# One fused kernel of attention and two feed-forward layers: weight splitting moved to GpSimd, gate splitting moved to VectorE, and a planner that counts a shared port

## The chip, the cores and the metric

The kernel runs on one core of one Trainium2 chip. The metric is the device time of one execution in microseconds (us), as the median of several runs. The engines are named as in the profile: PE (TensorE, matmul), PEld (its weight loads), DVE (VectorE), ACT (ScalarE), POOL (GpSimd) and SP (the queue that issues DMAs).

## The reference

```python
scores = scale * q @ k^T + bias(i, j)          # B=2, H=8, S=576, D=64
attn   = softmax(scores) @ v                   # -> x: 1152 tokens x 512
h = x @ w_in;  g = s * relu(h)**2 + b;  x = g @ w_out           # layer 1, 512 -> 2048 -> 512
h = x @ w_in;  g = h * tanh(log1p(exp(min(h, 20))));  out = g @ w_out   # layer 2, same sizes
```

The bias is a small two-layer network of the distance between positions. The weights arrive as 64-bit floats and are put together from two 32-bit words on the chip.

## The kernel before, in words

Every matmul of the two layers has 32-bit precision made of three products of a rounded format: each operand is taken apart into a high part (a rounding copy) and a low part (the operand minus the high part), and the product is high x high + low x high + high x low. So each weight block and each gate block needs a copy and a subtraction.

A layer is worked through as 48 tiles: three passes j of 384 tokens, and in each pass 16 blocks f of 128 hidden features. A tile has its hidden products (L788, 12 matmuls into a PSUM bank `h`, of which there are four), its gates, and its sums (L865, 12 matmuls in layer 1 and 9 in layer 2, added up over the pass in the PSUM banks `y`, of which there are four). Layer 1 uses four `y` banks in a pass, layer 2 three. The hidden products of a tile stand several tiles ahead of its sums on PE.

In layer 2 the gates of a tile are six DVE operations and three ACT operations in a chain: `least` (DVE, L806, reads PSUM), `exp` (ACT, L809), `both` (DVE, L813), `log` and `over` (ACT, L817, L820), then `one`, `times`, `newton`, `gate` (DVE, L823, L826, L829, L832); `times` is the last that reads the bank `h`. Then ACT makes the high part `gh` (L842) and POOL or DVE the low part `gl` (`minus`, L157). In layer 1 it is `relu` (ACT, L798), `square` (DVE, L801), `gh` (ACT) and `gl` (DVE).

The weights of layer 2 are prepared during the third pass of layer 1, 32 blocks of 128 x 512 (16 `wi` for the hidden products, 16 `wo` for the sums). For each: a DMA, `widen` (two ACT operations, L138 and L139), `join` (DVE, L144), `high` (a copy: on ACT for `wi`, on DVE for `wo`, L163), `low` (`minus` on DVE, L157). The buffer `wf` that `widen` fills has two copies each for `wi` and `wo` and comes free with `low`.

At the end of layer 1's last pass, `scaled_sum` (DVE, L876) reads the four `y` banks, which frees them for layer 2, and at the end of each pass of layer 2 `out_left` (ACT, L888) and `out_right` (DVE, L891) copy the sums out of their banks to `ob`.

The order of the instructions on every engine is set by a planner in the kernel (`Plan.run`): each operation is a task with a cost in us, a rank, what it comes after, and which buffers it holds. The planner starts the task that can start earliest. A task whose `port` is set can't overlap another such task: these are all of POOL's, and on DVE `bias_row` and `join`.

Of the kernel before, what the change touches and what calls it, by code (L numbers as in the profile page):

```python
# [10 lines left out]
F32 = mybir.dt.float32  # L11
# [10 lines left out]
def attention_bias_then_two_moe(ctx: ExitStack, tc: tile.TileContext, ins, out):  # L22
    nc = tc.nc
    q, k, v = ins["q"], ins["k"], ins["v"]
# [17 lines left out]
    NF = FF // P  # L42
    TB = 384
    NB = NT // TB
# [30 lines left out]
    HLEAD = 25  # L75
# [5 lines left out]
    DEAL = 6  # L81
    WEARLY = ("i0", "i1", "o0", "i2", "o1", "i3", "o2", "o3")
    FILL = 4
    LASTV = 2
    LXRANK = -78
    CUT = 0
    FRANK = 32
# [2 lines left out]
    GRANK = -190  # L90
    PRANK = -66
    VRANK = 1
    BIG = 3.0e38
    SD = S // DEAL
    scale = 1.0 / float(np.sqrt(D))
# [25 lines left out]
    class Weights:  # L121
# [26 lines left out]
            self.wlo = self.pool[0].tile([P, KD * P], F32R, tag=f"w{self.nm}l", name=f"wl{self.name}")  # L148
            copy(SPLIT["io".index(self.nm)], self.whi, self.wf.bitcast(F32))

        def low(self):
            minus(nc.vector, self.wlo, self.wf.bitcast(F32), self.whi)
            self.put[self.nm] = self.whi, self.wlo

    def minus(engine, out, x, y):

        engine.tensor_tensor(out, x, y.bitcast(F32), op=ALU.subtract)  # L157
# [338 lines left out]
    class Task:  # L496
        def __init__(self, engine, us, rank, f, args, after, takes, lag, mb):
            self.engine, self.us, self.rank, self.f, self.args = engine, us, rank, f, args
            self.after, self.takes, self.lag, self.mb = list(after), list(takes), lag, mb
            self.start = self.end = None  # L500
            self.behind, self.past = [], []

            self.port = engine == "POOL" or f.__name__ in ("bias_row", "join") and engine == "DVE"

    class Hold:
        def __init__(self, what):
# [2 lines left out]
    class Plan:  # L509
# [5 lines left out]
        def add(self, engine, us, rank, f, *args, after=(), takes=(), mb=0.0):  # L515
            t = Task(engine, us, rank, f, args, after, takes, self.LAGS[engine], mb)
            self.tasks.append(t)
            return t
# [60 lines left out]
    add = plan.add  # L579
# [24 lines left out]
    for x, G in enumerate(gorder):  # L604
        n, first, step = GFIRST
        at = -200 + 8 * x if x < NFIRST else 10 * (first + step * x if x < n else first + step * n + GSTEP * (x - n))
        w = side(G)[0]
        hs = [Hold("r") for a in range(RI)]
        rs = [
            add(*(("ACT", 0.0008 * w + 0.1) if row_engine(G, a) == "a" else ("DVE", 0.0007 * w + 0.05)), at - 15 + a,  # L610
                bias_row, G, a, after=[], takes=[hs[a]])
# [9 lines left out]
        for c0, c1 in bias_pieces(G):  # L621
            h1 = Hold("one")
            p = add("PE", 0.00167 * (c1 - c0) + 0.14, at, bias_products, G, c0, c1, after=rs, takes=[h1])
# [12 lines left out]
    for n, (key, i) in enumerate(firsts.items()):  # L636
        st = stacks[key]
        at = 10 * (i - QLEAD if n >= Q0 else -5 + n)
        packs = []
        for nm in "qk":  # L640
# [5 lines left out]
            who = "a" if n < PACK0 else "p"  # L646
# [4 lines left out]
        for what in range(3):  # L651
            h1 = Hold("one") if big is None or what == 2 else hold
            t = add("PE", 0.3 if what == 2 else 0.55, at + what, st.turn, what, big,
                    after=([packs[what][1]] if what < 2 else [p1 for _, p1 in packs]) + ts[-1:], takes=[] if h1 is hold and what else [h1])
            ts.append(t)
            if what == 2:
                for hn, _ in packs:
                    hn.users.append(t)
            who = PUTS[what]
            p = add(*(("ACT", 0.28 if what == 2 else 0.46) if who == "a" else ("DVE", 0.28 if what == 2 else 0.57)), at + what + 1,  # L660
                    st.put, what, who, after=[t, *puts[:1]])
# [7 lines left out]
    for i, u in enumerate(units):  # L669
        at = 10 * i  # L670
        if u.b == 0:
            for n in range(u.n):
                h = Hold("nb")
                after = [*issued[-1:], *([scored[i - NLEAD]] if i >= NLEAD else []), *(stores[G] for G in range(u.q0 // (RI * RI), (u.q0 + u.w) // (RI * RI)))]
                nbh[u.hp, u.t, n] = h, add("SP", 1.1 if u.both else 0.55, at - (80 if i > 1 else 400), load_bias, u.hp, u.t, u.heads(n), after=after,
                                           takes=[h], mb=0.29)
# [6 lines left out]
        for n in range(u.n):  # L683
            h, load = nbh[u.hp, u.t, n]
            hs = Hold("s")
# [13 lines left out]
        t = add("PE", 0.62 * u.n, at + RANK["turn"], u.turn, after=ds, takes=[hp, hr])  # L699
# [9 lines left out]
        p = add("PE", 1.24 if u.n == 2 else 0.73, at + RANK["V"], u.values, after=[kp, kr, valued[u.hp, u.b]], takes=[ho])  # L709
# [39 lines left out]
    whave, wused = {}, {}  # L749

    def add_w(L, f, nm, at, early):
        w = Weights(wpa if f < EARLY else wpb, L, f, nm)
        two = "2" if nm == "o" and not early else ""
        if two:
            def load():
                w.st = stg[1]
                w.load()
        else:
            load = w.load
        hr, hf, hw = Hold("wraw" + two), Hold("wf" + two), Hold(f"w{'a' if f < EARLY else 'b'}{nm}")  # L760
        new = [] if early else [opened]
        t = add("SP", 0.42, at - 20, load, after=[ended, *(new if two else [])], takes=[hr], mb=0.52)
        t = add("ACT", 1.12, at, w.widen, after=[t], takes=[hf])
        t = add("DVE", 0.6, at + 1, w.join, after=[t])
        hr.users.append(t)
        t = add(*(("ACT", 0.52) if SPLIT["io".index(nm)] == "a" else ("DVE", 0.34)), at + 2, w.high, after=[t, *new], takes=[hw])
        t = whave[L, f, nm] = add("DVE", 0.6, at + 3, w.low, after=[t])
        hf.users.append(t)
        wused[L, f, nm] = hw.users

# [126 lines left out]
    ready = {(0, j): lows[j] for j in range(NB)}  # L897
# [8 lines left out]
    for n, (L, j, f) in enumerate((L, j, f) for L in range(2) for j in range(NB) for f in range(NF)):  # L906
# [9 lines left out]
        if n < FILL:  # L916
            hs = []
            for c in range(KD):
                hs.append(add("PE", 0.53, 10 * (len(units) + FRANK + 5 * f), blk.hidden, (c,), after=[lasts, wi, *hs, *ready[L, j]],
                              takes=[] if c else [hh]))  # L920
        else:
            hs = [add("PE", 2.08, at - HLEAD, blk.hidden, after=[lasts, wi, *ready[L, j]], takes=[hh])]
        in_turn(hs[0], "h")
        wused[L, f, "i"] += hs
        if not WHOLE:
# [111 lines left out]
```

## Time and profile before

| What | us |
|---|---|
| median of 3 runs (618.38 to 619.24) | 618.52 |
| the profiled execution, whole | 619.38 |
| its span, first to last instruction | 617.6 |
| PE busy / DVE busy | 592.8 / 470.2 |
| ACT busy / POOL busy | 381.1 / 123.4 |

Attention takes the first 204 us of the span, layer 1 runs to about 416 us and layer 2 from there to the end. The granted PE clock is 0.999 of full speed. PE is at work 96% of the span. A line of the timeline gives start, duration, engine, line, operation, what it writes and reads and how many instructions are merged in it; in brackets stand the idle time of the engine before it and what ended that.

### The profile page before, as it was taken

Reading aid. Unit: us, or ns where it says so; the run is one execution under the profiler, and the core shown is the slowest. Engines: PE = TensorE matmul, PEld = TensorE weight load, DVE = VectorE, ACT = ScalarE, POOL = GpSimd, SP = SyncE. Lnnn points to the kernel's source line nnn. Section 1 sums busy time; section 2 is a strip of 40 time slices with the busy share of each in tenths; the row PEclk is TensorE's granted clock in tenths of the full one; section 3 lists DMA queues with packets and bytes.
Section 4 is the critical chain, followed back from the end, with each engine's and each line's share of the span. In section 5 each row is a group of like instructions: output and inputs, shape, how many; then the busy total and the mean of one; then the engine's idle time right before and its main releaser. Section 6 shows DMA issues by size and latency. Waiting matters only on the chain.

```text
span 617.6 us, 12029 instructions
## 1 busy us (share of the span) xinstructions
PE 592.8 (96%) x4416; PEld 520.7 (84%) x4416; DVE 470.2 (76%) x1048; ACT 381.1 (62%) x797; POOL 123.4 (20%) x183
## 2 busy tenths in 40 slices
PE   3988999999999999999999999999999999999996
PEld 1444687778888999999999999997898789989984
DVE  5999978877896699634223889899888777787885
ACT  3766877778998899623123788754555444545543
POOL 2223335343344000000000000001222212222120
PEclk9999999999999999999999999999999999999999
DMA  5786756646543678700000377420000100010001
GB/s 121 249 250 204 215 155 179 196 131 201 181 142 103 203 227 281 246 1 1 1 0 13 100 244 242 154 69 1 2 0 1 51 2 2 0 52 1 2 1 51
DMA packets 47083, 65.97 MB, mean 107 GB/s; under 512 B 12720, under 2 KB 32304, under 8 KB 47024
## 3 DMA queue, kind: packets, MB, share of 16 engines
q1 hardware_dynamic: 46688, 64.81, 34.2%
q8 instruction: 35, 0.57, 0.4%
q10 hardware_dynamic: 336, 0.39, 0.2%
q14 instruction: 24, 0.20, 0.1%
HBM read 51.93 MB, written 13.25 MB: 106 GB/s over the span
## 4 chain that ended last, share of the span: by engine, by line
PE 78%; DVE 14%; ACT 3%; DMA 2%; issue 2%; POOL 1%; SPq 0%; ACTq 0%; DVEq 0%
PE h L788 29%; PE y L865 28%; PE s L405 6%; PE po L467 6%; DVE r L257 5%; PE pp L446 5%; PE bias L267 3%; DMA rawq<-in_q_dram 2%; DVE s L415 1%; DVE r L829 1%; DVE u L823 1%; PE pr L448 1%; DVE n L826 1%; PE t L369 1%; DVE qk L163 1%
## 5 line engine op out<-in xcount | busy, mean ns | idle before, releaser
L157 POOL TENSOR_TENSOR gl<-n,gh 128x384 fp32r<-128x384 f32 x46 | 47.4, 1031 | 291.2 <-ACT gh L842 291.2
L437 POOL TENSOR_SCALAR e<-e,rs 128x576 f32<-128x576 f32 x72 | 55.9, 788 | 91.4 <-DVE rs L433 45.1
L257 DVE TENSOR_SCALAR r<-lx,bl 128x352 f32<-128x352 f32 (+17 forms) x144 | 66.6, 523 | 2.1 <-PE bias L267 1.7
L801 DVE SCALAR_TENSOR_TENSOR u<-h,u 128x384 f32<-128x384 f32 x48 | 26.6, 555 | 52.9 <-ACT u L798 52.8
L788 PE MATMUL h<-yh,wli 128*128 128x384 f32 x192 | 64.8, 337 | 0.0
L788 PE MATMUL h<-yh,whi 128*128 128x384 f32 x192 | 64.7, 337 | 0.0
L788 PE MATMUL h<-yl,whi 128*128 128x384 f32 x192 | 64.7, 337 | 0.0
L788 PE MATMUL h<-xh,whi 128*128 128x384 f32 x192 | 64.6, 336 | 0.0
L788 PE MATMUL h<-xh,wli 128*128 128x384 f32 x192 | 64.5, 336 | 0.0
L788 PE MATMUL h<-xl,whi 128*128 128x384 f32 x192 | 64.4, 336 | 0.0
L425 ACT ACTIVATE e<-s,mn 128x576 f32<-128x576 f32 x72 | 55.5, 772 | 9.7 <-DVE mn L415 7.0
L798 ACT ACTIVATE u<-h 128x384 f32<-128x384 f32 x48 | 23.3, 487 | 58.6 <-PE h L788 58.6
L415 DVE CUSTOM_DVE_ANT_0 s<-s,nb 128x576 f32<-128x576 f32 x72 | 52.4, 751 | 9.2 <-PE s L405 9.0
L817 ACT ACTIVATE r<-n,two 128x384 f32<-128x384 f32 x48 | 29.5, 614 | 38.9 <-DVE n L813 38.9
L823 DVE SCALAR_TENSOR_TENSOR u<-n,r 128x384 f32<-128x384 f32 x48 | 35.2, 733 | 23.0 <-ACT r L820 23.0
L405 PE MATMUL s<-qk 64*128 64x144 f32 (+1 forms) x640 | 49.6, 294 | 1.1 <-DVE mn L415 0.8
L405 PEld LDWEIGHTS s<-qk 64*128 64x128 f32 (+1 forms) x640 | 40.6, 176 | 10.4 <-issue 5.2
L865 PE MATMUL y<-who,gh 128*128 128x512 f32 x144 | 43.9, 399 | 4.5 <-ACT gh L842 1.6
L809 ACT ACTIVATE u<-u 128x384 f32<-128x384 f32 x48 | 25.0, 521 | 34.1 <-DVE u L806 34.1
L865 PE MATMUL y<-gl,who 128*128 128x384 f32 (+1 forms) x192 | 44.5, 338 | 0.0
L865 PE MATMUL y<-gh,wlo 128*128 128x384 f32 (+1 forms) x192 | 44.4, 337 | 0.0
L865 PE MATMUL y<-gh,who 128*128 128x384 f32 (+1 forms) x192 | 44.3, 337 | 0.0
(89 smaller groups left out, 1412.3 us busy)
## 6 DMA issues: line engine op xcount, KB each, us to landing
rawi<-in_moe_w_in_dram SPq DMA_DIRECT2D x32, 512.0 KB, 4.3
rawo<-in_moe_w_out_dram SPq DMA_DIRECT2D x32, 512.0 KB, 4.4
nbias_d<-bo SPq DMA_DIRECT2D x36, 295.5 KB, 2.9
nb<-nbias_d SPq DMA_DIRECT2D x32, 288.0 KB, 3.8
rawq<-in_q_dram SPq DMA_DIRECT2D x8, 288.0 KB, 5.8
rawk<-in_k_dram SPq DMA_DIRECT2D x8, 288.0 KB, 6.3
out_dram<-ob SPq DMA_DIRECT2D x9, 256.0 KB, 2.0
natv<-in_v_dram SPq DMA_DIRECT2D x16, 128.0 KB, 3.6
```

What stands on the lines that cost most here:

```text
L157: engine.tensor_tensor(out, x, y.bitcast(F32), op=ALU.subtract)
L257: engine.tensor_scalar(r, src, bl[:, g : g + 1], 0.0, op0=ALU.add, op1=ALU.max)
L405: nc.tensor.matmul(self.ps[rows, x if self.both else 2 * j + x, o : o + PIECE], st.qk[d, 0, self.q0 : self.q0 + self.w], st.qk[d, 1, c0 : ...
L415: nc.vector.tensor_tensor_reduce(out=self.s[n][:m], in0=self.ps[:m, 2 * n : 2 * n + 2, :HALF], in1=nb[:m].rearrange("p (n j) -> p n j", n= ...
L425: nc.scalar.activation(out=self.e[n][:m], in_=self.s[n][:m].rearrange("p n j -> p (n j)"), func=AF.Exp, bias=self.mn[n][:m], scale=-1.0, a ...
L437: nc.gpsimd.tensor_scalar(self.e[n][:m], self.e[n][:m], self.rs[:m, n : n + 1], 0.0, op0=ALU.mult, op1=ALU.add)
L446: nc.tensor.transpose(self.pp[:, n, c, :m], self.e[n][:m, c * P : c * P + P], ident[:m, :m])
L467: nc.tensor.matmul(self.po[D * j : D * j + D, :w], va[:, c, j, :], p, start=(c == 0), stop=(c == NQ - 1))
L788: nc.tensor.matmul(self.ph, w[:, c * P : (c + 1) * P], x[:, c, :], start=(c == 0 and n == 0), stop=(c == KD - 1 and n == 2),)
L817: nc.scalar.activation(out=self.r, in_=self.n, func=AF.Ln, bias=two)
L823: nc.vector.scalar_tensor_tensor(self.z, self.n, 2.0, self.r, op0=ALU.add, op1=ALU.mult)
L865: nc.tensor.matmul(o, a, c, start=(f == 0 and i == 0), stop=(f == NF - 1 and i == 2))
```

## The change

Four things are changed, the first of them in the planner alone.

- The planner sets `port` for `both`, `one`, `newton` and `gate` on DVE too.
- `low` of the weights: in layer 2 (`LOWS[1] = "pp"`) it runs on POOL, at a planned cost of 1.3; in layer 1 it stays on DVE.
- `LASTV` goes from 2 to 34: the low part `gl` of the last 34 tiles (tiles 14 and 15 of layer 2's first pass, and its second and third pass) runs on DVE, where it was on POOL for all but the last two.
- `TAIL = 15`: the hidden products of the last four tiles have a rank of 40 ahead of their sums (`HLEAD` of 25 plus 15), so four tiles where it was two and a half.

```diff
-    LASTV = 2
+    LASTV = 34
...
+    PORTS = ("bias_row", "join", "both", "one", "newton", "gate")
+
+    LOWS = ("vv", "pp")
+    TAIL = 15
...
-        def low(self):
-            minus(nc.vector, self.wlo, self.wf.bitcast(F32), self.whi)
+        def low(self, who):
+            minus(nc.gpsimd if who == "p" else nc.vector, self.wlo, self.wf.bitcast(F32), self.whi)
...
-            self.port = engine == "POOL" or f.__name__ in ("bias_row", "join") and engine == "DVE"
+            self.port = engine == "POOL" or engine == "DVE" and f.__name__ in PORTS
...
-        t = whave[L, f, nm] = add("DVE", 0.6, at + 3, w.low, after=[t])
+        who = LOWS[L]["io".index(nm)]
+        t = whave[L, f, nm] = add(*(("DVE", 0.6) if who == "v" else ("POOL", 1.3)), at + 3, w.low, who, after=[t])
...
-            hs = [add("PE", 2.08, at - HLEAD, blk.hidden, after=[lasts, wi, *ready[L, j]], takes=[hh])]
+            hs = [add("PE", 2.08, at - HLEAD - (TAIL if n >= 2 * NB * NF - 4 else 0), blk.hidden, after=[lasts, wi, *ready[L, j]], takes=[hh])]
```

The order on all engines is the same as before up to the third pass of layer 1. From there it differs in many places; three follow. A name such as `h1_0_4` is the bank of layer 2 (numbered 1), pass 0, block 4; `y1_0_2` is the sum of layer 2, pass 0, third bank; the last number is a buffer's. Five lines added ahead shift the line numbers: L865 is L870 in the change, L157 is L161.

**DVE at the seam of the two layers.** The rows from the copy of the last but one `wo` to the third `scaled_sum` (`y32_2_e`), before:

```order
L163 CAST who_1_14_5547<-wfo_1_14_5478 128x512
L876 TENSOR_SCALAR y32_2_0_5552<-y0_2_0_4731,s_sb_71,bw_73 128x384
L157 TENSOR_TENSOR wlo_1_14_5548<-wfo_1_14_5478,who_1_14_5547 128x512
L832 TENSOR_TENSOR n1_0_1_5500<-n1_0_1_5500,r1_0_1_5505 128x384
L157 TENSOR_TENSOR yl2_5551<-y32_2_0_5552,yh2_5550 128x384
L163 CAST who_1_15_5584<-wfo_1_15_5528 128x512
L806 TENSOR_SCALAR u1_0_3_5588<-h1_0_3_5464 128x384
L157 TENSOR_TENSOR wlo_1_15_5585<-wfo_1_15_5528,who_1_15_5584 128x512
L876 TENSOR_SCALAR y32_2_1_5592<-y0_2_1_4781,s_sb_71,bw_73 128x384
L813 SCALAR_TENSOR_TENSOR n1_0_2_5594<-u1_0_2_5526 128x384
L157 TENSOR_TENSOR yl2_5551<-y32_2_1_5592,yh2_5550 128x384
L876 TENSOR_SCALAR y32_2_2_5605<-y0_2_2_4812,s_sb_71,bw_73 128x384
```

and in the change:

```order
L167 CAST who_1_14_5535<-wfo_1_14_5469 128x512
L837 TENSOR_TENSOR n1_0_1_5472<-n1_0_1_5472,r1_0_1_5479 128x384
L881 TENSOR_SCALAR y32_2_0_5546<-y0_2_0_4729,s_sb_71,bw_73 128x384
L148 SCALAR_TENSOR_TENSOR wfo_1_15_5523<-rawo_1_15_5447,wfo_1_15_5523 128x512
L161 TENSOR_TENSOR yl2_5545<-y32_2_0_5546,yh2_5544 128x384
L167 CAST who_1_15_5571<-wfo_1_15_5523 128x512
L881 TENSOR_SCALAR y32_2_1_5579<-y0_2_1_4761,s_sb_71,bw_73 128x384
L818 SCALAR_TENSOR_TENSOR n1_0_2_5595<-u1_0_2_5515 128x384
L161 TENSOR_TENSOR yl2_5545<-y32_2_1_5579,yh2_5544 128x384
L881 TENSOR_SCALAR y32_2_2_5600<-y0_2_2_4789,s_sb_71,bw_73 128x384
```

The subtractions `wlo` are gone from this queue; on POOL they now stand between the first `gl` of layer 2 (`wlo_1_13`, `gl1_0_0`, `wlo_1_14`, `gl1_0_1`, `wlo_1_15`, `gl1_0_2`). On PE the hidden products `h1_0_4` have gone from ahead of the last two blocks of layer 1's sums to between layer 1's last sum and layer 2's first; `h1_0_5` still follows that first sum.

**PE at the seam of layer 2's first and second pass.** One row of a group of three or twelve; before:

```order
L865 MATMUL y1_0_2_5609<-who_1_15_5584,gl1_0_15_6107 128x512
L865 MATMUL y1_1_0_6197<-who_1_0_4861,gh1_1_0_6146 128x512
L865 MATMUL y1_1_0_6197<-who_1_0_4861,gl1_1_0_6147 128x512
L865 MATMUL y1_1_1_6206<-who_1_0_4861,gh1_1_0_6146 128x512
L788 MATMUL h1_1_4_6233<-yl1_4721,whi_1_4_4802 128x384
```

and in the change:

```order
L870 MATMUL y1_0_2_5609<-who_1_15_5571,gl1_0_15_6122 128x512
L870 MATMUL y1_1_0_6189<-who_1_0_4838,gh1_1_0_6157 128x512
L870 MATMUL y1_1_0_6189<-who_1_0_4838,gl1_1_0_6158 128x512
L793 MATMUL h1_1_4_6200<-yl1_4718,whi_1_4_4816 128x384
L870 MATMUL y1_1_1_6223<-who_1_0_4838,gh1_1_0_6157 128x512
```

The twelve hidden products of tile 4 have moved ahead of the second sum of the new pass. At the next seam, of the second and third pass, `h1_2_3` has moved the other way: from ahead of the three first sums to behind them.

**PE at the end.** One row of a group of three, six or twelve; before:

```order
L788 MATMUL h1_2_14_7227<-yl2_5551,whi_1_14_5282 128x384
L865 MATMUL y1_2_0_6814<-who_1_11_5410,gl1_2_11_7207 128x512
L865 MATMUL y1_2_0_6814<-who_1_12_5456,gh1_2_12_7245 128x512
L788 MATMUL h1_2_15_7266<-yl2_5551,whi_1_15_5311 128x384
L865 MATMUL y1_2_0_6814<-who_1_12_5456,gl1_2_12_7246 128x512
```

and in the change:

```order
L793 MATMUL h1_2_14_7214<-yl2_5545,whi_1_14_5290 128x384
L870 MATMUL y1_2_0_6794<-who_1_11_5394,gh1_2_11_7209 128x512
L793 MATMUL h1_2_15_7255<-yl2_5545,whi_1_15_5337 128x384
L870 MATMUL y1_2_0_6794<-who_1_11_5394,gl1_2_11_7210 128x512
L870 MATMUL y1_2_0_6794<-who_1_12_5444,gh1_2_12_7240 128x512
```

The hidden products of the last tile, and of the three before it, stand nine matmuls of a sum further ahead.

## Rows read from the trace of the kernel before

**Rows 1.** Busy time of the engines in two stretches, with instruction counts
```profile
core 0: us, PE busy (x) PEld busy (x) DVE busy (x) ACT busy (x) POOL busy (x), PEclk, DMA share, GB/s
345.00:412.00 67.00, 67.00 (x385) 67.00 (x385) 58.91 (x110) 51.91 (x101) 0.00 (x0) 1.00 0.56 173
491.00:541.00 50.00, 50.00 (x252) 45.16 (x251) 37.23 (x70) 24.62 (x48) 11.93 (x12) 1.00 0.00 1
```

**Rows 2.** Timeline of PE at the seam of the two layers
```profile
419.43 0.50 PE L865 MATMUL y<-who,gh 128*128 128x512 f32 x1 [0.43 <-DVE y L876]
...
420.00 0.40 PE L865 MATMUL y<-who,gl 128*128 128x512 f32 x1
421.29 0.50 PE L865 MATMUL y<-who,gh 128*128 128x512 f32 x1 [0.89 <-DVE y L876]
```

**Rows 3.** Timeline of PE at the seam of layer 2's first two passes
```profile
483.74 0.40 PE L865 MATMUL y<-who,gl 128*128 128x512 f32 x1
485.67 0.51 PE L865 MATMUL y<-who,gh 128*128 128x512 f32 x1 [1.53 <-DVE ob L891]
```

**Rows 4.** Timeline of PE at the end
```profile
604.11 0.86 PE L865 MATMUL y<-who,gl 128*128 128x512 f32 x3
...
607.70 0.96 PE L865 MATMUL y<-who,gh 128*128 128x512 f32 x3 [0.65 <-ACT gh L842]
...
611.05 0.50 PE L865 MATMUL y<-who,gh 128*128 128x512 f32 x1 [0.99 <-ACT gh L842]
```

**Rows 5.** The chain that ended last, two tiles' worth in layer 2's third pass
```profile
593.74 2.11 PE h L788 x12
595.86 2.10 PE y L865 x9
```

**Rows 6.** Groups of DVE instructions from 336 to 412 us: count, busy, mean ns
```profile
L157 DVE TENSOR_TENSOR wli<-wfi,whi 128x512 fp32r<-128x512 f32 x15 | 10.3, 687 | 0.0
L144 DVE SCALAR_TENSOR_TENSOR wfi<-rawi,wfi 128x512 int32<-128x512 int32 x14 | 9.7, 692 | 4.2 <-ACT rawi L139 4.1
...
L163 DVE CAST who<-wfo 128x512 fp32r<-128x512 f32 x14 | 5.9, 421 | 0.8 <-PE y L865 0.8
```

**Rows 7.** POOL's gate subtractions: all of them as one group, and two in the timeline
```profile
L157 POOL TENSOR_TENSOR gl<-n,gh 128x384 fp32r<-128x384 f32 x46 | 47.4, 1031 | 291.2 <-ACT gh L842 291.2
...
417.23 1.01 POOL L157 TENSOR_TENSOR gl<-n,gh 128x384 fp32r<-128x384 f32 x1 [3.71 <-ACT gh L842]
...
603.24 1.02 POOL L157 TENSOR_TENSOR gl<-n,gh 128x384 fp32r<-128x384 f32 x1 [2.24 <-ACT gh L842]
```

**Rows 8.** Timeline of DVE at the seam of the two layers
```profile
414.79 0.67 DVE L876 TENSOR_SCALAR y<-y,s_sb,bw 128x384 f32<-128x384 f32 x1
...
417.72 1.07 DVE L157 TENSOR_TENSOR wlo<-wfo,who 128x512 fp32r<-128x512 f32 x1
418.71 0.67 DVE L876 TENSOR_SCALAR y<-y,s_sb,bw 128x384 f32<-128x384 f32 x1
...
420.56 0.68 DVE L876 TENSOR_SCALAR y<-y,s_sb,bw 128x384 f32<-128x384 f32 x1
```

**Rows 9.** Timeline of DVE at the seam of layer 2's first two passes
```profile
481.83 0.56 DVE L832 TENSOR_TENSOR n<-n,r 128x384 f32<-128x384 f32 x1
...
485.19 0.42 DVE L891 COPY ob<-y 128x256 f32<-128x256 f32 x1
```

**Rows 10.** Timeline of DVE and of ACT in the last tiles
```profile
603.61 1.06 DVE L823 SCALAR_TENSOR_TENSOR u<-n,r 128x384 f32<-128x384 f32 x1 [1.09 <-ACT r L820]
604.60 0.54 DVE L806 TENSOR_SCALAR u<-h 128x384 f32<-128x384 f32 x1
605.07 0.54 DVE L826 SCALAR_TENSOR_TENSOR n<-n,h 128x384 f32<-128x384 f32 x1
...
606.57 0.62 ACT L817 ACTIVATE r<-n,two 128x384 f32<-128x384 f32 x1 [0.87 <-DVE n L813]
607.55 0.51 ACT L820 ACTIVATE r<-r 128x384 f32<-128x384 f32 x1
```

## The prediction

> **What bounds the kernel now.** I read the table of stretches first. It shows PE at work without a break from 345 to 412 us and from 491 to 541 us [rows 1]; a tile takes PE 2.11 for its hidden products and 2.10 for its sums, 4.2 us together [rows 5]. So in a layer's steady part PE is the bound, and a change that leaves PE's 4416 matmuls as they are can win only where PE stands still. The timeline of PE shows three such places behind attention, and the reader is to see in each what ended the wait.
>
> At the seam of the two layers PE waits 0.43 and then 0.89 for `scaled_sum` on DVE to free a `y` bank [rows 2]; nine matmuls of a sum in 2.10 start 0.23 apart, and the second wait makes 1.29 of that, so the two cost 0.43 + 1.06 = 1.5 us. At the seam of layer 2's first two passes it waits for `out_right` on DVE, and 1.93 stands where 0.23 would: 1.7 us [rows 3]. At the end it waits 0.65 and 0.99 for the last gates' high parts: 1.6 us [rows 4]. The sum is 4.8 us, the most that the change can give but for restarts (the first matmul behind each wait is some 0.1 longer, 0.50 for 0.40 [rows 2]). Attention and the first two passes of layer 1 keep their order on every engine, so nothing is won or lost ahead of 340 us.
>
> **The end.** In the change the last tile's hidden products come nine matmuls earlier: they end at 604.11 - 2.10 = 602.0, and behind them stand 0.7 (the rest of block 11) and four sums of 2.1 (blocks 12 to 15). So the sums of block 14 begin 4.9 us behind the last hidden products, those of block 15 7.0. Are the gates there by then? DVE starts an operation 0.47 behind the one before it (604.60 and 605.07) where nothing holds it; ACT's `log` takes 0.62 and its others about 0.5 [rows 10]. In the change's order the last tile runs: `least` 0.6, `exp` 0.55, `both` behind two operations of the tile before, done at 2.0; `log` and `over` to 3.2; `one` 3.7; then the `gl` of tile 14, `times`, `newton`, `gate` to 5.7; `gh` 6.2, `gl` 6.8. That is 0.8 ahead of block 15's sums, and tile 14's `gh` comes at about 3.7, 1.2 ahead of its own. The walk has no wait for POOL, since POOL now has nothing to do there; before, `one` was held by it to 1.06 us [rows 10] while POOL's subtraction ran [rows 7]. So I take the whole 1.6 off. If the walk is 1.5 too short, 0.7 of that stays.
>
> **The seam of layer 2's passes.** Twelve matmuls of `h1_1_4` (2.1 us) now stand ahead of the second sum, so PE asks for the bank 2.1 later. Before, the bank came at 485.67, 1.7 late. The copy that frees it (485.19) stood behind the `one` and `times` of tile 2; in the change it stands behind the `gate` of tile 1, which before was over by 482.4 [rows 9]. The wait goes: -1.7. `h1_1_4` needs the bank of `h1_1_0`, whose `times` lies before that `gate`. At the next seam `h1_2_3` no longer covers the copies: the second sum of the third pass now asks for its bank 2.8 us behind the end of the bank's own sum. In between come ACT's half and DVE's half of the copy, 0.4 each [DVE's: rows 9]. I cost that at nothing; if DVE stands as it did at the seam before (bank free 485.6, its sum over nine matmuls ahead of 483.74 [rows 3], by 482.0, so 3.6), it costs 0.8.
>
> **The two last passes.** `gl` moves to DVE for 34 tiles where it was there for two: one more operation of 0.47 per tile. DVE was busy 37.23 us for 12 tiles, 3.1 per tile [rows 1]; with 0.47 more it is 3.6, of 4.2. It also loses the wait for POOL, up to 0.5 per tile. DVE stays off the path; cost nothing, cover 0.6 per tile.
>
> **The weights of layer 2.** DVE loses 32 subtractions of 0.69 [rows 6], 0.60 each in its queue, 19 us in all. But DVE is not the bound in that stretch (58.91 of 67 busy, PE full [rows 1]), so this gives nothing by itself. POOL gets them. Their price is not in the trace: POOL's subtraction of 384 columns takes 1.03 [rows 7], so one of 512 takes between 1.03 (length costs nothing) and 1.37 (in proportion); I take 1.3, nearer to proportion, since DVE's own go 0.55 to 0.69. What matters is that the two engines exclude each other: DVE's subtraction at 417.72 took 1.07 where 0.69 is free [rows 8, 6], and ended 0.55 behind the end of POOL's (418.24 [rows 7]); `one` did the same at 603.61. From that one, POOL gives way about 0.1 ahead of its end, so I count 1.2 held.
>
> In that stretch a tile of 4.2 us meets two `join`s (0.60 each), a `who` copy (0.34, if it needs the port), a `gl` of layer 1 (0.47) and two of POOL's: 1.2 + 0.34 + 0.47 + 2.4 = 4.4 us of port. The planner counts only `join` and POOL's. So DVE and POOL fall 0.2 a tile behind for the nine or so tiles in which both kinds of weights are made, about 2 us; then, with `wo` alone (2.6 a tile), they recover. PE doesn't feel it there: with four `h` banks it asks for a tile's bank three tiles, 12.6 us, behind that tile's hidden products, and `relu` and `square` need little over 1 us of that. Behind a late POOL, `widen` on ACT waits for its `wf` buffer, and `relu` and `gh` queue behind it; those have the same slack.
>
> **The seam of the layers.** This is where lateness would show. PE's hidden products `h1_0_4` now fill 2.1 us between layer 1's last sum and layer 2's first, so the last sums end 2.1 earlier and `scaled_sum` can start at about 412.7 where it stood at 414.79 [rows 8], while PE asks for the second bank as before at 419.0, for the third at 419.7. From the first `scaled_sum` to the end of the third the change has ten operations, 5 us, less the two `wlo` that stood there, plus the holds by POOL: three of its operations fall there, for which I count half, 1.7. From 412.7 that ends at 419, in time; before it ended at 421.2 (the last of [rows 8]). If DVE arrives 2 us late, the third bank is 1.1 late. I take that: 1.5 of waits becomes 1.1, -0.4. Bounds: no wait (-1.5) and, if port time is 0.5 a tile more than counted, +5.
>
> The sum: -1.6 - 1.7 - 0.4 = -3.7, with 0.2 for restarts -3.9. The profiled execution took 619.38, so 615.5; it lies 0.86 above the median, so for the median **614.6 us**.
>
> **The rivals.** *The port is the bound (slower).* If POOL's subtraction holds the port for its whole 1.37 and each change of holder costs another 0.1, a tile needs 2.75 + 2.0 + 0.4 = 5.2 us of port for 4.2 of PE. Over 12 tiles DVE is 12 us late; 1 is slack and some 3 is recovered with `wo` alone, so PE stands 8 us at the layers' seam where it stood 1.5: +6.5 - 3.3 - 0.2 = +3.0, 621.5. The change is slower than before from about 0.8 late per tile on. For it: `wlo` at 1.07; nothing in the trace shows long runs of such neighbours. Against: with `wo` alone it recovers, and `who` waits for PE's sums of the same block anyway. The Trainium skill has a rule on this side: "Perfetto Trace Analysis", section Optimizing Scalar/DVE Operations, warns that moving work between GpSimd and DVE may not help, as they share a read port. By that rule the 19 us that DVE loses come back as waits. The trace agrees as far as the exclusion goes (1.07 for 0.69).
>
> *DVE becomes the bound of the last passes.* DVE idled (50 - 37.23) / 12 = 1.06 a tile [rows 1], in waits for ACT inside the chain. If these stay whole, seven operations of 0.47 and they make 4.35, above 4.2: over 31 tiles 4.7 late, which eats the lead and the gain at the end. Then -1.7 - 0.4: 616.4.
>
> *The waits only move.* DVE has been full at the layers' seam, and PE could wait for the gates of the next tiles in place of the banks. Then each seam keeps its loss: 618.2, no change.
>
> **How the numbers follow.** Forecast 0.62 (613.0 to 616.0 by itself), port 0.14, DVE in the last passes 0.14, waits that move 0.10. A measurement can tell about 0.2%, 1.2 us. Faster: nearly all of the first and most of the third, 0.72; same 0.14; slower 0.14, the port. The range goes from 612.4 (all waits and restarts gone, 1.1 more) to 619.2 (waits that move, and the port's mild cases).
>
> **What would show it.** Right: PE's wait of 1.53 for `ob` gone, the last wait for `gh` gone, the last two passes at 4.2 a tile, `wli` and `wlo` on POOL near 1.3, and a wait for `scaled_sum` of 1 us or less at the seam. Wrong: POOL busy without a break from 345 to 420, DVE's `join` and `gl` near 1 us, and a wait of several us at the first sums of layer 2; or sums of the last passes waiting for `gl` on DVE.

## The result, and the profile after

The changed kernel takes 623.58 us (median of 4 runs, 623.35 to 623.82) where the kernel before took 618.88 beside it (618.38 to 619.46). The ratio is 1.0076, with a 95% interval of 1.0058 to 1.0093: slower by 0.8%, where 614.6 was predicted, faster, with a range that ended at 619.2. The profiled span is 621.6 us, before it was 617.6.

The table of stretches answers to [rows 1]. Columns: stretch, its length, busy time of PE, weight loads, DVE, ACT and POOL (instructions), PE's granted clock, DMA share, GB/s.

```profile
345.00:412.00 67.00, 66.76 (x381) 66.05 (x379) 57.01 (x70) 47.79 (x92) 38.60 (x25) 1.00 0.52 165
491.00:541.00 50.00, 50.00 (x253) 45.20 (x252) 43.05 (x87) 26.43 (x51) 0.00 (x0) 1.00 0.04 17
```

In the last passes DVE now has 43.05 of 50 us where it had 37.23, and PE is still full: that part went as predicted. In layer 1's third pass PE is nearly full too, POOL has gone from 0 to 38.60 us, and DVE, with 40 instructions fewer in this window (70 for 110), is busy almost as long (57.01 for 58.91). It got rid of a third of its operations and of next to none of its time.

PE's timeline at the seam of the two layers answers to [rows 2]. Columns, as in all timelines here: start, duration, engine, line, operation, and in brackets the idle time before it and who ended it.

```profile
412.36 0.44 PE L870 MATMUL y<-gh,who 128*128 128x384 f32 x1 [0.55 <-ACT gh L847]
...
415.52 0.44 PE L793 MATMUL h<-yh,whi 128*128 128x384 f32 x1 [0.47 <-DVE n L831]
...
423.27 0.80 PE L870 MATMUL y<-who,gh 128*128 128x512 f32 x1 [5.37 <-DVE y L881]
...
424.72 0.52 PE L793 MATMUL h<-yh,whi 128*128 128x384 f32 x1
425.04 0.52 PE L793 MATMUL h<-yl,whi 128*128 128x384 f32 x1
...
428.56 0.62 PE L870 MATMUL y<-who,gh 128*128 128x512 f32 x1
...
429.48 0.39 PE L870 MATMUL y<-who,gh 128*128 128x512 f32 x1
```

The sum into the third bank began at 421.29 before [rows 2], now at 429.48, 8.2 us later. PE stands (sits idle) for 5.37 us behind one `scaled_sum`, where it stood 0.43 and 0.89, with two short stands ahead of it. Behind the stand the twelve products of a tile take 428.56 - 424.72 = 3.84 us for 2.11 [rows 5]: they start 0.32 apart, not 0.17 to 0.18. The table of stretches for the seam shows why:

```profile
418.00:423.00 5.00, 0.00 (x0) 0.00 (x0) 4.89 (x9) 2.96 (x6) 1.88 (x3) 0.92 0.00 2
423.00:429.00 6.00, 5.73 (x17) 5.35 (x18) 5.91 (x9) 2.51 (x6) 3.46 (x3) 0.50 0.01 3
429.00:435.00 6.00, 6.00 (x30) 5.28 (x29) 5.17 (x10) 2.98 (x7) 1.02 (x1) 1.00 0.00 0
```

PE has done nothing from 418 to 423, and in the next 6 us the granted clock is 0.50, the lower of its two levels (1.2 GHz); by 429 it is back at 2.4.

DVE's three sums answer to [rows 8]:

```profile
422.55 0.67 DVE L881 TENSOR_SCALAR y<-y,s_sb,bw 128x384 f32<-128x384 f32 x1
...
425.85 0.67 DVE L881 TENSOR_SCALAR y<-y,s_sb,bw 128x384 f32<-128x384 f32 x1
...
428.21 0.68 DVE L881 TENSOR_SCALAR y<-y,s_sb,bw 128x384 f32<-128x384 f32 x1
```

The first is at 422.55 where it stood at 414.79 and was predicted at 412.7. DVE comes 8 us late to the seam, 10 against the forecast. From there to the end of the third sum it takes 428.89 - 422.55 = 6.3 us, as long as the forecast had it (412.7 to 419); so the lateness is made ahead of the seam. Where from, the groups from 336 to 412 us show, the answer to [rows 6] (columns: group, count, busy time, mean ns of one, idle time before them and who ended it); the last two, POOL's, are from 336 to 432:

```profile
L161 DVE TENSOR_TENSOR gl<-u,gh 128x384 fp32r<-128x384 f32 x16 | 18.2, 1137 | 1.7 <-ACT gh L847 1.7
L167 DVE CAST who<-wfo 128x512 fp32r<-128x512 f32 x12 | 12.2, 1016 | 0.3 <-PE y L870 0.3
L148 DVE SCALAR_TENSOR_TENSOR wfi<-rawi,wfi 128x512 int32<-128x512 int32 x14 | 11.6, 825 | 2.5 <-ACT rawi L143 2.2 <-issue 0.4
L148 DVE SCALAR_TENSOR_TENSOR wfo<-rawo,wfo 128x512 int32<-128x512 int32 x12 | 11.5, 962 | 2.4 <-ACT rawo L143 1.2 <-issue 1.1
L806 DVE SCALAR_TENSOR_TENSOR u<-h,u 128x384 f32<-128x384 f32 x15 | 8.3, 554 | 5.3 <-ACT u L803 5.2
...
L161 POOL TENSOR_TENSOR wlo<-wfo,who 128x512 fp32r<-128x512 f32 x16 | 24.9, 1558 | 18.3 <-DVE who L167 18.3
L161 POOL TENSOR_TENSOR wli<-wfi,whi 128x512 fp32r<-128x512 f32 x15 | 22.3, 1485 | 22.3 <-ACT whi L165 14.8 <-DVE u L806 7.4
```

The copy `who` takes 1016 ns in the mean where it took 421, `join` of `wfo` 962 and of `wfi` 825 where 692 stood, layer 1's `gl` 1137 where one takes 0.55 unhindered. Only `square`, which reads one operand from PSUM, keeps its 554. POOL's own operations take 1485 and 1558 in the mean, and 1.29 us where nothing of DVE's holds them.

One tile of this stretch, one of the longest, all engines that matter, the changed kernel:

```profile
395.60 0.56 DVE L806 SCALAR_TENSOR_TENSOR u<-h,u 128x384 f32<-128x384 f32 x1 [0.62 <-ACT u L803]
396.07 0.68 DVE L148 SCALAR_TENSOR_TENSOR wfi<-rawi,wfi 128x512 int32<-128x512 int32 x1
396.67 1.54 DVE L167 CAST who<-wfo 128x512 fp32r<-128x512 f32 x1
398.13 0.68 DVE L148 SCALAR_TENSOR_TENSOR wfo<-rawo,wfo 128x512 int32<-128x512 int32 x1
398.74 1.64 DVE L161 TENSOR_TENSOR gl<-u,gh 128x384 fp32r<-128x384 f32 x1
401.00 0.56 DVE L806 SCALAR_TENSOR_TENSOR u<-h,u 128x384 f32<-128x384 f32 x1 [0.62 <-ACT u L803]
...
396.17 1.76 POOL L161 TENSOR_TENSOR wli<-wfi,whi 128x512 fp32r<-128x512 f32 x1 [1.60 <-ACT whi L165]
398.29 1.68 POOL L161 TENSOR_TENSOR wlo<-wfo,who 128x512 fp32r<-128x512 f32 x1 [0.37 <-DVE who L167]
...
400.47 0.49 ACT L803 ACTIVATE u<-h 128x384 f32<-128x384 f32 x1 [2.85 <-DVE gl L161]
```

And DVE's in the kernel before, at the same place:

```profile
389.40 0.55 DVE L801 SCALAR_TENSOR_TENSOR u<-h,u 128x384 f32<-128x384 f32 x1
389.87 0.42 DVE L163 CAST who<-wfo 128x512 fp32r<-128x512 f32 x1
390.32 0.69 DVE L144 SCALAR_TENSOR_TENSOR wfi<-rawi,wfi 128x512 int32<-128x512 int32 x1
390.93 0.69 DVE L157 TENSOR_TENSOR wlo<-wfo,who 128x512 fp32r<-128x512 f32 x1
391.53 0.55 DVE L157 TENSOR_TENSOR gl<-u,gh 128x384 fp32r<-128x384 f32 x1
392.00 0.68 DVE L157 TENSOR_TENSOR wli<-wfi,whi 128x512 fp32r<-128x512 f32 x1
392.93 0.69 DVE L144 SCALAR_TENSOR_TENSOR wfo<-rawo,wfo 128x512 int32<-128x512 int32 x1 [0.25 <-ACT rawo L139]
393.54 0.55 DVE L801 SCALAR_TENSOR_TENSOR u<-h,u 128x384 f32<-128x384 f32 x1
```

Before, `square` returns after 393.54 - 389.40 = 4.14 us, PE's own pace. Now it returns after 5.40: 0.47 `square`, 0.60 `join`, 1.46 for a copy that got stuck behind POOL's `wli` (begun at 396.17), 0.61 `join`, 1.64 for a `gl` behind POOL's `wlo` (begun 398.29), and 0.62 in which DVE waits for `relu`. `relu` stood 2.85 us on ACT for the `u` buffer that this very `gl` gives back. Two low halves (1.2 us) went; two holds (the copy 1.12 longer, `gl` 1.17) and the wait came.

Not every tile is that long. The first and the last `square` of ten tiles, before:

```profile
360.36 0.55 DVE L801 SCALAR_TENSOR_TENSOR u<-h,u 128x384 f32<-128x384 f32 x1
...
401.04 0.55 DVE L801 SCALAR_TENSOR_TENSOR u<-h,u 128x384 f32<-128x384 f32 x1
```

and of the same ten in the change:

```profile
355.19 0.56 DVE L806 SCALAR_TENSOR_TENSOR u<-h,u 128x384 f32<-128x384 f32 x1 [0.94 <-ACT u L803]
...
405.78 0.56 DVE L806 SCALAR_TENSOR_TENSOR u<-h,u 128x384 f32<-128x384 f32 x1 [0.62 <-ACT u L803]
```

Before, a tile took DVE (401.04 - 360.36) / 10 = 4.07 us, now (405.78 - 355.19) / 10 = 5.06, and three in a row near the end 5.4. DVE begins these ten 5.2 us ahead of the kernel before and ends them 4.7 behind it; on the way to the first scaled sum it loses another 3.0.

From 345 us to the end of the third scaled sum, instruction by instruction: DVE's work shrinks by 19 us, 28 of its operations are held (last over 0.15 us longer than their kind does alone) for 24 us in all, and its idle time grows by 3 us. That makes 8 us more, the lateness of the seam.

The other two places of loss are gone. The pass seam [rows 3] and the end [rows 4] in PE's timeline now, with no bracket on them:

```profile
489.45 0.39 PE L870 MATMUL y<-who,gl 128*128 128x512 f32 x1
489.68 0.40 PE L870 MATMUL y<-who,gh 128*128 128x512 f32 x1
...
614.91 0.40 PE L870 MATMUL y<-who,gh 128*128 128x512 f32 x1
```

PE's balance: from 400 us on it stands 6.39 us in all where it stood 4.49 (+1.9), and the lower clock costs 0.65 in the first three sums' matmuls, 1.73 in the products and 0.2 in the next sums (+2.6). That is 4.5; its last matmul ends 3.6 later (617.17 for 613.54), in an execution that was 0.6 ahead at 321 us. Most of the 2.6 is not a loss of its own: DVE frees the third bank only at 428.89, so at the full clock PE could have begun that sum at most 0.6 earlier and would have stood instead.

### The profile page after: what moved, and what is told of

It is laid out like the page before. It is cut to its first block, busy times and chain, and to the rows that moved or that the text cites. A ratio compares the mean times of both kernels' runs of the same rounds, so it can differ in the third digit from the quotient of the medians.

```text
span 621.6 us, 12013 instructions
## 1 busy us (share of the span) xinstructions
PE 594.1 (96%) x4416; PEld 523.3 (84%) x4416; DVE 483.7 (78%) x1048; ACT 384.7 (62%) x797; POOL 140.7 (23%) x183
## 4 chain that ended last, share of the span: by engine, by line
PE 76%; DVE 12%; ACT 4%; issue 3%; DMA 2%; POOL 2%; SPq 0%; DVEq 0%; ACTq 0%; POOLq 0%
PE h L793 28%; PE y L870 28%; PE s L409 6%; PE po L471 6%; DVE r L261 5%; PE pp L450 5%; PE bias L271 3%; DMA rawq<-in_q_dram 2%; DVE s L419 1%; POOL wlo L161 1%; DVE gl L161 1%; DVE who L167 1%; PE pr L452 1%; PE t L373 1%; DVE qk L167 1%
## 5 line engine op out<-in xcount | busy, mean ns | idle before, releaser
L870 PE MATMUL y<-who,gh 128*128 128x512 f32 x144 | 43.8, 399 | 5.4 <-DVE y L881 5.4
L870 PE MATMUL y<-gh,who 128*128 128x384 f32 (+1 forms) x192 | 44.6, 338 | 0.6 <-ACT gh L847 0.6
L870 PE MATMUL y<-gl,who 128*128 128x384 f32 (+1 forms) x192 | 44.6, 339 | 0.1
L870 PE MATMUL y<-gh,wlo 128*128 128x384 f32 (+1 forms) x192 | 44.4, 337 | 0.0
L161 POOL TENSOR_TENSOR wli<-wfi,whi 128x512 fp32r<-128x512 f32 x16 | 23.6, 1473 | 91.6 <-ACT whi L165 84.2
L870 PE MATMUL y<-wlo,gh 128*128 128x512 f32 x144 | 43.5, 397 | 0.0
```

What stands on the lines that cost most here:

```text
L870: nc.tensor.matmul(o, a, c, start=(f == 0 and i == 0), stop=(f == NF - 1 and i == 2))
```

## The experiments

Theory P: POOL's 32 subtractions hold something, here called the port, which VectorE's operations on two SBUF operands, and its copies, need too. Rivals: the new order of the program delays the seam (O); POOL's results come too late for those who wait for them (D). Ratios are to the kernel before, run on the same chip beside each.

**POOL's subtractions back on VectorE** (low_v), all else as changed:

```diff
-    LOWS = ("vv", "pp")
+    LOWS = ("vv", "vv")
```

> Edit: of the change all is kept but POOL's weight subtractions, which go back to VectorE. Theory P (POOL's 32 subtractions hold a port that VectorE's joins, copies and low halves need, so VectorE is late at the seam of the two layers): the 5.4 us stand of PE at the seam shrinks to 0 to 2 us, the granted clock stays at 1.00 there, and the gains at the pass seam (1.7) and at the end (1.6 to 2.3) stay: about 615, 613.5 to 616.5. Rival O (the new order of the program, from the planner's added gate ports and the four earlier products, is what delays the first sums of layer 2): PE still stands 4 us or more at the seam, 621 to 624.

615.2 us (613.9 to 615.98), ratio 0.9923 [0.9905, 0.9941]: *faster* than before by 0.8%. Behind 333 us PE stands once for more than 0.2, at the seam:

```profile
421.92 0.50 PE L870 MATMUL y<-who,gh 128*128 128x512 f32 x1 [1.28 <-DVE y L881]
```

The granted clock is 1.00 there. So the order, the gate ports and the earlier products are not what costs; O falls as the main cause. All that the prediction hoped for is here, and POOL's subtractions take some 9 us from it (1.0076 against 0.9923).

**POOL's subtractions alone** (only_low_p), all else as before:

```diff
-    LASTV = 34
+    LASTV = 2
-    PORTS = ("bias_row", "join", "both", "one", "newton", "gate")
+    PORTS = ("bias_row", "join")
-    TAIL = 15
+    TAIL = 0
```

> Edit: of the change only POOL's weight subtractions for layer 2 are kept; gates' low halves on POOL as before, the planner's old list of port users, no earlier products at the end. Theory P: the loss at the seam of the layers (about 8 us) comes without the gains (about 4 us): 627, range 624 to 631, with a stand of PE of 4 us or more behind a first sum of layer 1's third pass. Rival O: the time of the kernel before within 1 us, 618 to 620. Rival D (POOL's product comes too late for who needs it: each low half takes 1.3 to 1.7 us instead of 0.7 and waits behind the other in order): also slower, but PE or ACT wait for wli, wlo at the seam and VectorE's joins, copies and gates' low halves keep the lengths that they had before.

627.79 us, ratio 1.0134 [1.0118, 1.0150]. PE stands 5.3 us at the seam behind `scaled_sum`, and 2.1 ahead of it. Held operations are as long as in the change: from 336 to 412 us `gl` takes 1139 ns in the mean (1137 in the change), the copy `who` 1014 (1016), where D has them keep their lengths. The loss is 8.4 us here, without the gains.

**POOL's operations without a consumer** (spare_read), on the kernel before; the planner does not count them as users of the port:

```diff
         def low(self):
             minus(nc.vector, self.wlo, self.wf.bitcast(F32), self.whi)
             self.put[self.nm] = self.whi, self.wlo
 
+        def spare(self):
+            nc.gpsimd.tensor_tensor(void, self.whi.bitcast(F32), self.whi.bitcast(F32), op=ALU.subtract)
...
+        if L == 1:
+            add("POOL", 1.3, at + 3, w.spare, after=[t])
```

> Edit: the kernel before, where POOL in addition subtracts each of layer 2's 32 weight tiles (128x512) from itself into a tile that nobody reads; nobody waits for POOL, and the orders of PE, ACT and VectorE are those of before but for a few rows at the seam. Theory P: POOL's operations alone make VectorE's joins, copies, low halves and gates' low halves of the third pass longer (mean 0.9 to 1.4 us instead of 0.42 to 0.69), and as VectorE keeps its own 32 low halves (22 us) the loss is larger than the change's: a stand of PE of 6 us or more at the seam, 627 to 640. Rival D (POOL's result is late, not VectorE): nobody needs this result, 618 to 620, VectorE's operations as long as before.

633.93 us, ratio 1.0233 [1.0218, 1.0248]. DVE is busy 16.00 of 16 us from 385 to 401, and a tile takes it 398.99 - 393.62 = 5.37 us. DVE, then POOL:

```profile
393.62 0.55 DVE L809 SCALAR_TENSOR_TENSOR u<-h,u 128x384 f32<-128x384 f32 x1
394.09 0.41 DVE L169 CAST who<-wfo 128x512 fp32r<-128x512 f32 x1
394.42 0.68 DVE L144 SCALAR_TENSOR_TENSOR wfi<-rawi,wfi 128x512 int32<-128x512 int32 x1
395.02 1.52 DVE L163 TENSOR_TENSOR wlo<-wfo,who 128x512 fp32r<-128x512 f32 x1
396.47 1.39 DVE L163 TENSOR_TENSOR gl<-u,gh 128x384 fp32r<-128x384 f32 x1
...
398.99 0.55 DVE L809 SCALAR_TENSOR_TENSOR u<-h,u 128x384 f32<-128x384 f32 x1
...
394.64 1.35 POOL L156 TENSOR_TENSOR void<-who 128x512 bf16<-128x512 f32 x1 [2.57 <-DVE who L169]
396.08 1.37 POOL L156 TENSOR_TENSOR void<-whi 128x512 bf16<-128x512 f32 x1
```

Nobody reads `void`, so nothing waits for a result, and still VectorE's `wlo` takes 1.52 and `gl` 1.39: each ends 0.4 to 0.55 behind the POOL operation that had begun before it, as if it had started only then. D falls as the main cause, and with DVE idle nowhere from 385 to 401 us, holds alone make a tile 5.4. PE, too, stands here, 0.9 us a tile behind `square`: with DVE at 5.4, PE is no longer the bound of this stretch.

**Half of them** (in_p), the weights into the hidden layer on POOL:

```diff
-    LOWS = ("vv", "pp")
+    LOWS = ("vv", "pv")
```

> Edit: the change, with half of POOL's subtractions: the weights into the hidden layer on POOL (16), those out of it on VectorE (16). Theory P with a limit: port time per tile of layer 1's third pass is 1.3 for POOL and 3.0 for VectorE (two joins 1.4, copy 0.4, low half 0.7, gate's low half 0.55), 4.3 beside a tile of 4.2 on PE, where the change has 4.9; so VectorE gets late by some 2 us, not 8: 616 to 618.5. If the loss went by the number of POOL's operations (half of the 8.4 us between the change and the run with all of them on VectorE): 619 to 620.

616.77 us, ratio 0.9983 [0.9974, 0.9993], in P's range. `square` comes back every 4.67 us (393.43, 398.11), less than the 5.40 with both but still above 4.2; one operation of the tile is held (`gl`, 1.66), where two are in the change. PE stands 2.40 at the seam. By the ratios half of the operations cost 3.7 us, all of them 9.5: somewhat under half, but with intervals of some 1 us on each ratio it isn't shown that the loss grows faster than their number.

**The planner told of everything** (allports), the change with

```diff
-            self.port = engine == "POOL" or engine == "DVE" and f.__name__ in PORTS
+            self.port = engine == "POOL" or engine == "DVE" and (f.__name__ in PORTS or f.__name__ in ("low", "high", "low_sum") and rank > 900)
```

> Edit: the change as it is, with the planner told of the other users of the port too (after attention VectorE's copies and all subtractions of low halves). Theory P: what is short is the port's time, not the planner's knowledge of it: the order of the port's users changes, but VectorE is still late at the layers' seam and PE stands 3 us or more there, 620 to 625. Rival O: the loss comes from an order that the planner laid out blind, and with the full list it mends: 615 to 617.5.

620.77 us, ratio 1.0047 [1.0025, 1.0069]. PE stands 2.67, 1.24 and 1.41 at the seam, 5.3 in all, in pieces; of the 16 `gl` from 336 us on 11 are held, at 1.56 in the mean (10 at 1.41 in the change). By the ratios this order gives back about 2 us of the 9, though the two intervals overlap; the planner, told of the port, does not win back the rest.

**The products ahead of the sums** (h_ahead), the change with layer 2's fifth block ahead:

```diff
+        if (L, j, f) == (1, 0, 5):
+            for y in firsty:
+                y.behind = y.behind + hs
...
+        if (L, j, f) == (1, 0, 0):
+            firsty = ys
```

> Edit: the change, with the 12 products of layer 2's block 5, first pass, put ahead of the four first sums of that pass on PE, so that they run within the 5.4 us in which PE stood; nothing else moves. Theory S (what sets the seam is when VectorE gives back the sums' banks, its third scaled_sum ends at 428.9 in the changed kernel's profile; the products at the lower clock only fill the time up to there): block 1's sums start at about 429.6 instead of 430.2, the time falls by 0.3 to 1 us, to about 623. Rival C (the twelve products at the lower clock, 3.8 us for 2.1, and the clock after the stand are on the path): 2 to 3.5 us less, 620 to 621.5.

623.52 us, ratio 1.0095 [1.0081, 1.0109]: no gain. PE's timeline:

```profile
423.84 0.50 PE L870 MATMUL y<-who,gh 128*128 128x512 f32 x1 [1.39 <-DVE y L881]
...
427.12 0.80 PE L870 MATMUL y<-who,gh 128*128 128x512 f32 x1 [2.31 <-DVE y L881]
...
429.48 0.79 PE L870 MATMUL y<-who,gh 128*128 128x512 f32 x1 [0.71 <-DVE y L881]
```

C's 2 to 3.5 us did not come. The sum into the third bank still begins at 429.48, now held up by the third scaled sum on DVE (0.71), as S says. But S's gain of 0.3 to 1 us did not come either: DVE was itself 0.5 later with that sum, and the clock fell in this run too (0.51 from 426 to 429), now under the sums behind the banks. What the lower clock costs by itself this run does not separate.

**The parts of the gain**, each taken out of low_v or alone on the kernel before.

Out of low_v (low_v_tail0):

```diff
-    TAIL = 15
+    TAIL = 0
```

> Edit: the run with POOL's weight subtractions back on VectorE (615.2 us), and in addition the products of the last four tiles led as early as all others. By the prediction's term the wait at the end comes back: 1.6 us more, 616.8 (616.2 to 618), with PE's last waits for gh. If the gate ports or the moved gates' low halves cured the end, not this edit: 615 to 615.6.

616.01 us, ratio 0.9965 [0.9954, 0.9975]. One wait is back, 1.57 us for `gh`; by the ratios the edit is worth 2.6 us, with intervals of some 1 us on each.

Out of low_v (low_v_lastv2), and out of the change (lastv2):

```diff
-    LASTV = 34
+    LASTV = 2
```

> Edit: as low_v, and the gates' low halves of layer 2's last passes back on POOL. By the prediction's term (these cost VectorE nothing and gain nothing) 615.2 (614.4 to 616). If POOL's low halves in the last passes were what made VectorE late at the end and at the pass seam, those waits come back: 617 to 618.5.

> Edit: the change, with the gates' low halves of layer 2's second and third pass back on POOL (all but the last two). Theory P as to the seam of the layers: nothing changes there (PE stands 5 us). If VectorE carries these low halves at no cost, as the prediction said, the time is that of the change or more, 623 to 625.5; if they cost VectorE what it lacks, the last passes get shorter than 4.2 us per tile and the time falls to 621 to 622.5.

613.57 us, ratio 0.9930 [0.9914, 0.9947], beside 0.9923 for low_v; and 623.94, 1.0074 [1.0059, 1.0089], beside 1.0076 for the change. Gates' low halves on VectorE or on POOL in the last passes: no difference, in either surrounding.

Out of low_v (low_v_oldports):

```diff
-    PORTS = ("bias_row", "join", "both", "one", "newton", "gate")
+    PORTS = ("bias_row", "join")
```

> Edit: as low_v, with the planner's old list of port users (no gate operations in it). By the prediction's term the product h of the pass seam falls behind the second sum again and the wait of 1.5 us for ob comes back: 616.9 (616.2 to 617.6). If the pass seam was cured by something else: 614.8 to 615.8.

614.07 us, ratio 0.9945 [0.9925, 0.9964]; the wait for `ob` comes back with 0.38 us, not 1.5. A miss: without the list, most of that wait is gone too. What else differs from the kernel before is the gates' low halves, which are off POOL, and `TAIL`, which acts on the last four tiles; so the low halves are the likely cure.

The new list alone (only_ports), the kernel before with:

```diff
+    PORTS = ("bias_row", "join", "both", "one", "newton", "gate")
...
-            self.port = engine == "POOL" or f.__name__ in ("bias_row", "join") and engine == "DVE"
+            self.port = engine == "POOL" or engine == "DVE" and f.__name__ in PORTS
```

> Edit: the kernel before, with nothing but the four gate operations in the planner's list of port users. By the prediction's term the product of the pass seam gets ahead of the second sum and the wait of 1.5 us for ob goes: ratio to before 0.9972 (1.7 us less), the two waits at the end (1.6 us) and the one at the layers' seam stay. Rival: the pass seam needs the gates' low halves off POOL as well, or is cured by them alone: within 0.5 us of before.

615.47 us, ratio 0.9957 [0.9942, 0.9972]. The wait for `ob` is gone; PE's waits behind 400 us sum to 2.75 where they were 4.49, 1.74 less, 1.53 of it the wait for `ob`. So either edit removes all or most of this wait.

**A try at the last wait** (sums_act): low_v_lastv2 with the third pass's scaled sums on ScalarE.

```diff
+        if j == NB - 1:
+            nc.scalar.activation(out=y, in_=py[0, j, e][:, :TB], func=AF.Identity, bias=bw[:, e : e + 1], scale=s_sb)
+        else:
+            nc.vector.tensor_scalar(y, py[0, j, e][:, :TB], s_sb, bw[:, e : e + 1], op0=ALU.mult, op1=ALU.add)
...
-                    t = add("DVE", 0.6 + 0.13 * (j == 0), at + e, scaled_sum, j, e, after=[ys[e], *ready[1, j][-1:]], takes=[hu])
+                    t = add("ACT" if j == NB - 1 else "DVE", 0.6 + 0.13 * (j == 0), at + e, scaled_sum, j, e, after=[ys[e], *ready[1, j][-1:]], takes=[hu])
```

> Edit: weights' low halves on VectorE, gates' low halves on POOL but for the last two (as low_v_lastv2), and the four scaled sums of layer 1's third pass on ScalarE, reading PSUM with the scale and the bias as vectors. If the last wait of PE (1.3 us behind the third scaled sum) is VectorE's queue: it goes or shrinks under 0.5, 0.8 to 1.3 us less than low_v_lastv2, a ratio to before of 0.991. If ScalarE's own queue puts the sums as late (it waits for the gates of the tiles between): the ratio stays at 0.993 or rises.

613.67 us, ratio 0.9933 [0.9921, 0.9946]: nothing. The wait of 1.3 behind `scaled_sum` is gone, and 1.50 stands in its place, behind a `times` on DVE that frees an `h` bank:

```profile
419.74 0.44 PE L793 MATMUL h<-yh,whi 128*128 128x384 f32 x1 [1.50 <-DVE n L831]
```

low_v, low_v_lastv2 and sums_act can't be told apart, and all three beat both kernels, by 0.7 to 0.8% and by 1.4 to 1.5%.

## Why the prediction was wrong

**The end, -1.6: right.** The waits are gone in the change, and one of 1.57 comes back without the edit.

**The pass seam, -1.7: right in place and size** (the wait of 1.53 goes with the list alone), though the list is not the only cure. No wait came at the next seam, which had been costed at nothing.

**Gates' low halves on DVE, 0: right.** DVE's busy time rose by 5.8 us for 12 tiles, 0.48 a tile as costed, under PE's 4.2. The rival that made DVE the bound of the last passes is out.

**POOL's price, 1.3: right for an operation by itself.** The shortest take 1.28 to 1.30. In the mean they take 1.49 and 1.56, since DVE holds POOL as well, and that was not in the sum.

**The port, and the seam of the layers, -0.4: this is the step that failed.** The prediction wrote "1.2 + 0.34 + 0.47 + 2.4 = 4.4 us of port", had DVE "fall 0.2 a tile behind for the nine or so tiles", 2 us, "then, with `wo` alone (2.6 a tile), they recover". Measured are 5.06 us a tile over ten tiles, 1.0 more than the same ten took before, 5.4 in the longest, and no recovery: the last `square` of layer 1 is 4.7 us later than before (405.78 for 401.04), the first scaled sum 7.8. The hold was costed rightly (1.2; 1.12 and 1.17 measured), and so was DVE's stretch from the first scaled sum to the end of the third (6.3). Three other things were wrong.

It added up port time as if both engines could always use the port when it was free. But DVE works in order: while its copy is held, the `square` and `join` behind it stand too, and while DVE runs them or waits for ACT, POOL's next operation may have nothing to read yet. POOL idles 1.60 and 0.37 us of the tile shown, and the tile is long all the same. What decides is the length of DVE's own queue: its work (0.47 + 0.60 + 0.34 + 0.60 + 0.47 = 2.5 us), holds of 1.12 and 1.17, nearly the whole length of POOL's operation, and the wait of 0.62: 5.4.

It gave `relu` "the same slack" as PE. `relu` needs one of two `u` buffers, which the held `gl` gives back, so the hold runs once round ACT and returns to DVE as 0.62 us of idle time in such a tile.

And the recovery did not come. Behind the last `square` POOL still runs five `wlo`, from 406.75 to 426.01, each waiting for DVE's copy `who`, in among the gates and the scaled sums of the seam. They hold DVE there too (`join` 1.63 at 406.96, `one` 1.65 at 416.89), and so does POOL's first `gl` of layer 2 (`newton` 1.30 at 419.86).

**The rival that came true** was the port, at a chance of 0.14: it had 5.2 us a tile, a stand of 8 us and 621.5. The sign was right, and the sizes came close: 5.06 us a tile, 6.4 us of stands, 623.6. The way there was in part luck: it had the port in use without a break, where POOL idles 2 us of the tile shown, and it had 3 us recovered, where 3.0 more were lost. The stand behind the scaled sum is shorter (5.37), and the clock was not in the sum. The rule that the prediction cites beside it (the Trainium skill, "Perfetto Trace Analysis", section Optimizing Scalar/DVE Operations: moving work between GpSimd and DVE might not help) agrees with this trace: 19 us left DVE and 24 came back as holds. What spoke against it there, the recovery with `wo` alone, was the wrong sentence. The chance was too low for a case whose turning point (0.8 late per tile) lay between its own price per tile and the forecast's (5.2 and 4.4, for 4.2 of PE).

**That the waits only move** did not happen where POOL stays out: low_v has 1.28 us of waits for 4.49.

## What to carry to other kernels

An operation that two engines exclude each other from is not free on the idle one. Count in the queue of the busy engine what leaves it and what each hold adds, at nearly the whole length of the other's operation; in the tile shown 0.6 us left and 1.1 to 1.2 came, twice. A planner that knows such a port only for some of its users can be told of the others, but here that took back at most some 2 us of 9. Leaving the subtractions where they were was the better choice (0.9923 against 1.0076); no run tried them on a third engine.

A dummy operation whose result nobody reads, on the engine that is suspected, tells a shared resource from a late result in one run.

## What the runs showed of the hardware

What is held and what is not: a cast copy of one SBUF operand (`who`, 0.42 alone, up to 1.54), and the operations on two SBUF operands that come behind one of POOL's (`join` up to 1.79, `gl` and `one` up to 1.65, `both` 1.26, `newton` 1.30) wait for POOL; `square`, `least`, `times` and the scaled sums, which read PSUM, keep their 0.55 and 0.67 while POOL runs. That the copy is among the held was not expected: the prediction left it open ("if it needs the port"). The Trainium skill, "SBUF — State Buffer", section "Who interferes with whom", says just this: two SBUF inputs, or a copy in a mode with two ports, exclude a GpSimd operation that reads SBUF, one SBUF input does not, and who comes first keeps the ports for the whole instruction. The trace agrees for the two inputs, for the one input and for who comes first (where `join` at 396.07 came first, POOL's `wli` took 1.76 for 1.29); that this copy runs in such a mode no run here shows, only that it is held.

A stand of PE can bring its clock down, but its length alone does not tell. In the change the granted clock was 0.50 for some 7 us, from within the stand of 5.37 to 429 us. It also fell behind stands of 2.67 (allports; products 0.17 apart up to 418.28, 0.32 apart from 418.46, a microsecond and a half behind the restart) and 2.40 (in_p), and stayed at 1.00 behind 1.28 (low_v), 1.50 (sums_act), and 2.78 in spare_read:

```profile
421.76 0.44 PE L796 MATMUL h<-yh,whi 128*128 128x384 f32 x1 [2.78 <-DVE n L834]
```

Before, with 0.43 and 0.89 at this seam, it was 1.00 throughout. What such a fall costs in time isn't shown. Of in_p's ten executions the five with a mean granted clock of 0.997 or less took 615.81 to 616.93 us, the five with 0.999 or more 616.40 to 618.69: those with the lower clock were not the longer ones.
